# Block-causal attention with a gated convolution unit: q and k loads split in 112 and 16 partitions, and a new hand-written order

## The chip, the cores and the metric

The kernel runs on one core of a Trainium2 chip. The core has five engines that run side by side, each through its own list of instructions in order: TensorE (PE, matmuls; PEld is its weight load), VectorE (DVE), ScalarE (ACT), GpSimd (POOL) and SyncE (SP). Here SP issues nearly all DMAs. The engines wait for each other by semaphores. The metric is the device time of one execution in microseconds, as the median of the runs shown.

## What is computed

Attention over 8 batches, 8 heads, 576 positions and head size 64, where position i sees every position in its own block of 64 and in earlier blocks; then a gated unit on the joined heads (512 columns): a causal convolution of five taps gives a gate, a matrix gives a value, and a second matrix projects gate times value.

```python
scores = scale * np.matmul(q, k.transpose(0, 1, 3, 2))
mask = block_i >= block_j
attn = softmax(np.where(mask, scores, -1e9))
x = np.matmul(attn, v)                      # heads joined: [8, 576, 512]
for t in range(5):
    gate_pre += conv_w[t][None, None, :] * xp[:, t:t + 576, :]
gate = 1.0 / (1.0 + np.exp(-gate_pre))
out = (gate * (x @ w_val)) @ w_out
```

(The softmax is written out in the original; the rest is cut to its core.) Inputs and output are float32; the kernel computes in float16 with float32 sums.

## The kernel before

All work is cut into some 800 steps, and their order is written out by hand as two strings of words, START and PLAN. A loop (`run`, L458) walks through the words and calls one helper for each, so the order of words is the order of instructions on every engine at once: an engine executes those of its own in that order. Nothing is reordered later, and the waits for data and for free buffers follow from the order.

A word is a name, numbers, and behind an @ either the engine (A is ACT, D is DVE, P is POOL) or the PSUM banks. The numbers are a head group Q (0 to 15: batch Q // 2, four heads of it), a batch, or a unit of 512 output rows (8 and 9 are the rests of four batches each).

- `Lq.Q`, `Lk.Q` (L175 to L185) load q or k of a head group, 576 KB on 128 partitions with 4,608 bytes each, into one of three buffers `qks`, so the load for Q needs the casts of Q - 3 done. `Lv.b.c`, `Lvt.b` load v and its tail (256 and 128 KB in pieces of 256 bytes); `Lwv`, `Lwo`, `Lcw` the weights.
- `cq.Q.i` casts k (i = 1) or q (i = 0) to float16; a third number means a part: 0 the first five ninths, 1 the last four. `cv`, `cvt` cast v. `T.Q.i` transposes in blocks of 32 x 32 on DVE.
- `s.Q.t` computes scores (three pieces t per head group), `e.Q.t.a` is exp on ACT, `m` sets the masked corners to zero on POOL; `sl` and `el` do the last rows. `av` multiplies with v on TensorE, `n.Q.a` divides by the sum on DVE.
- x has to be transposed for the second part, in 32 pieces p = 2Q + a, either by `xtr.p` (five TensorE transposes) and `xt.p` (a copy out of PSUM), or by `dx.p`, a DMA that transposes, issued by SP. `tt` copies the ends.
- `cn` (80 small matmuls) is the convolution, `th` its tanh, `val`, `gv` and `o` value, gating and projection, `oc` the copy out of PSUM and `st` the store, issued by SP.
- `w` is a filler matmul on zeros, put where TensorE would wait.

SP walks through loads, `dx` and stores in the order of the words. So a load that stands behind a store is issued only when that store's data is there.

The load of q and k before (L175 to L179):

```python
def load_qk(i, src, Q, m):
    b, g = divmod(Q, 2)
    eng(m, nc.sync).dma_start(
        out=qks[Q % NQS][0:128, i],
        in_=src[b, 4 * g:4 * g + 4].rearrange("h (i n) d -> (h i) (n d)", n=18))
```

Of the kernel before, what the change touches and what calls it, by code (L numbers as in the profile page):

```python
# [19 lines left out]
el.0.1 s.1.0@0123 e.1.1.1 av.0.0@67 cq.2.1@P e.1.0.0 n.0.0 e.1.0.1 s.1.2@0145 m.1.1 cq.2.0@P T.2.1  # L20
av.0.1@67 e.1.2.1 xtr.0@2 e.1.2.0 m.1.0 T.2.0 cq.3.1@P xt.0@A n.0.1 w@3 w@3 w@3 s.2.1@0145 m.1.2
cq.3.0@P av.1.1@23 e.2.1.0 T.3.1 Lq.4 Lwv.0 e.2.1.1 s.2.2@0167 n.1.1 Lv.1.3 e.2.2.1 av.1.0@45 m.2.1
Lv.1.2 T.3.0 e.2.2.0 s.2.0@2367 n.1.0 cv.1.0@P e.2.0.1 xtr.3@0 xtr.1@1 xt.3@D xtr.2@4 e.2.0.0 m.2.2
xt.1@D xt.2@D w@5 sl.1@0167 cq.4.0@P s.3.0@2345 el.1.1 Lvt.1 el.1.0 e.3.0.0 cn.0@0167 Lk.4 tt.0
wv.0@D Lwo.1 wv.2@P T.4.0 e.3.0.1 Lq.5 val.0.0@2 Lwo.0 wv.3@A wv.1@D Lwo.3 m.2.0 m.3.0 Lk.5
val.0.1@3 th.0.0 cv.1.1@P Lwo.2 Lv.3.1 th.0.1 s.3.2@0145 gv.0.0 Lv.2.0 cvt.1@P gv.0.1 e.3.2.1
av.2.0@67 cq.4.1@P e.3.2.0 av.2.1@23 n.2.0 s.3.1@0145 m.3.2 n.2.1 xtr.4@6 e.3.1.0 val.0.3@7 cq.5.0@P
T.4.1 e.3.1.1 xtr.5@2 val.0.2@3 gv.0.3 xt.4@A m.3.1 xt.5@D s.4.1@0145 gv.0.2 av.3.1@67 e.4.1.1 T.5.0
cq.5.1@P Lv.2.1 e.4.1.0 s.4.2@2345 n.3.1 e.4.2.1 av.3.0@01 Lq.6 wo.0@D wo.1@P Lk.7 e.4.2.0 T.5.1
Lvt.2 s.4.0@4567 Lk.6 m.4.1 n.3.0 xtr.7@2 Lv.2.2 m.4.2 e.4.0.1 o.0.3@3 Lv.2.3 e.4.0.0 xt.7@D  # L30
sl.2@0167 oc.0.3@D cv.2.0@P o.0.1@2 el.2.0 el.2.1 xtr.6@3 m.4.0 oc.0.1@A s.5.2@0145 xt.6@D cq.6.0@P
cn.1@2367 e.5.2.1 e.5.2.0 tt.1 T.6.0 val.1.2@4 cq.7.1@P th.1.1 o.0.2@5 th.1.0 m.5.2 Lv.4.0 gv.1.2
cvt.2@P s.5.0@0167 T.7.1 oc.0.2@A cq.6.1@P val.1.0@4 Lv.3.0 e.5.0.0 val.1.1@5 gv.1.0 e.5.0.1 Lq.7
T.6.1 s.5.1@0123 Lk.8 cv.2.1@P val.1.3@4 Lv.3.3 e.5.1.0 gv.1.1 st.0.3 m.5.0 av.4.0@67 Lk.9 e.5.1.1
gv.1.3 Lv.4.3 s.6.1@0145 n.4.0 m.5.1 cv.3.0@P av.5.0@23 e.6.1.0 xtr.8@6 e.6.1.1 n.5.0 o.1.3@7
cq.7.0@P xt.8@A s.6.2@0145 oc.1.3@D st.0.1 xtr.10@2 m.6.1 e.6.2.0 T.7.0 Lvt.3 o.1.2@3 cq.8.1@P Lvt.4
xt.10@A s.6.0@0167 oc.1.2@D e.6.2.1 o.1.1@2 T.8.1 e.6.0.0 m.6.2 av.5.1@45 oc.1.1@D Lv.5.1 e.6.0.1
av.4.1@01 n.5.1 cq.9.1@P s.7.2@2367 n.4.1 Lq.8 o.1.0@4 e.7.2.0 m.6.0 st.0.2 Lv.4.2 xtr.9@5 e.7.2.1
oc.1.0@D s.7.1@0123 cvt.3@P Lv.3.2 xt.9@D xtr.11@4 cvt.4@P e.7.1.1 o.0.0@5 xt.11@D m.7.2 tt.2
e.7.1.0 sl.3@2367 oc.0.0@D el.3.1 T.9.1 s.7.0@0145 m.7.1 el.3.0 cn.2@2367 e.7.0.0 Lq.9 cq.8.0@P  # L40
Lv.4.1 e.7.0.1 val.2.0@0 Lk.10 T.8.0 th.2.0 Lv.5.0 m.7.0 cv.4.1@P val.2.2@1 th.2.1 gv.2.0 s.8.1@2345
cv.3.1@P val.2.3@0 gv.2.2 e.8.1.1 Lq.11 av.7.0@67 st.1.3 e.8.1.0 gv.2.3 cq.9.0@P st.1.2 s.8.2@0145
Lq.10 n.7.0 Lv.5.3 av.6.1@23 e.8.2.1 cv.4.0@P T.9.0 av.6.0@67 e.8.2.0 m.8.1 Lk.11 n.6.1 cq.10.1@P
dx.14 sl.4@0145 n.6.0 el.4.0 el.4.1 m.8.2 s.9.2@0123 val.2.1@4 T.10.1 e.9.2.0 dx.12 av.7.1@67
cq.11.0@P e.9.2.1 gv.2.1 s.8.0@0145 n.7.1 cv.5.0@P o.2.0@2 e.8.0.1 T.11.0 m.9.2 o.2.2@3 e.8.0.0
dx.15 cq.10.0@P oc.2.0@D s.9.1@4567 Lk.13 oc.2.2@A xtr.13@0 e.9.1.1 o.2.1@1 xt.13@D m.8.0 T.10.0
e.9.1.0 s.9.0@2367 Lv.6.2 oc.2.1@D e.9.0.0 cq.11.1@P av.8.1@45 e.9.0.1 Lv.5.2 s.10.0@0123 n.8.1
m.9.1 e.10.0.0 av.8.0@67 m.9.0 T.11.1 e.10.0.1 s.10.1@0145 tt.3 n.8.0 e.10.1.1 av.9.1@23 m.10.0
# [1 line left out]
st.2.2 cv.5.1@P val.3.0@1 Lk.12 th.3.0 gv.3.3 Lvt.5 cn.8@2367 Lv.7.1 gv.3.0 st.0.0 val.3.1@0 Lq.14  # L50
th.8.1 th.8.0 s.11.1@4567 gv.3.1 val.8.1@1 e.11.1.1 Lv.7.0 val.3.2@0 gv.8.1 e.11.1.0 cq.12.0@P
s.11.0@2367 gv.3.2 o.2.3@1 e.11.0.1 m.11.1 T.12.0 o.3.2@0 e.11.0.0 cq.12.1@P Lk.14 oc.2.3@D
sl.5@4567 oc.3.2@A dx.19 av.9.0@23 el.5.1 st.2.3 el.5.0 cvt.5@P T.12.1 s.10.2@0167 Lq.13 m.11.0
o.3.3@4 e.10.2.0 n.9.0 o.3.1@5 e.10.2.1 Lvt.7 T.13.1 s.11.2@0123 dx.18 oc.3.1@A cq.14.0@P val.8.2@6
oc.3.3@D e.11.2.1 val.8.0@5 gv.8.2 val.8.3@4 m.10.2 e.11.2.0 gv.8.0 s.12.1@2367 T.14.0 Lv.6.3
e.12.1.0 av.10.1@01 m.11.2 gv.8.3 cq.14.1@P e.12.1.1 av.11.1@45 n.10.1 s.12.0@2367 m.12.1 T.14.1
o.8.0@0 e.12.0.0 dx.16 n.11.1 o.8.1@1 e.12.0.1 cq.13.0@P dx.21 oc.8.0@D s.14.0@2345 oc.8.1@A Lv.6.0
av.11.0@67 e.14.0.1 m.12.0 T.13.0 o.3.0@0 e.14.0.0 st.8.1 n.11.0 cv.6.1@P Lv.7.3 av.10.0@45 oc.3.0@A
m.14.0 sl.6@2367 tt.4 n.10.0 dx.22 cv.7.0@P el.6.1 el.6.0 s.14.2@0167 dx.23 cn.4@2345 cvt.7@P
e.14.2.0 dx.20 e.14.2.1 val.4.1@0 Lv.7.2 th.4.0 m.14.2 val.4.3@1 th.4.1 gv.4.1 s.13.1@2367 Lv.6.1  # L60
# [7 lines left out]
el.7.1 s.15.1@0145 dx.26 n.13.1 o.5.1@6 e.15.1.1 dx.27 o.5.0@7 e.15.1.0 oc.5.1@D s.15.0@2345 st.5.1
oc.5.0@D m.15.1 av.14.1@01 e.15.0.0 st.5.0 av.14.0@67 e.15.0.1 n.14.1 tt.6 val.6.3@2 n.14.0 m.15.0
dx.29 av.15.1@01 dx.28 av.15.0@45 n.15.1 val.6.1@3 n.15.0 dx.31 cn.6@0167 dx.30 val.6.0@4 th.6.1  # L70
val.6.2@5 th.6.0 gv.6.3 o.5.2@6 gv.6.2 tt.7 gv.6.0 val.7.1@2 oc.5.2@A gv.6.1 val.9.0@7 st.5.2
val.9.3@3 cn.9@0145 o.6.3@6 th.9.1 th.9.0 gv.9.3 o.6.0@4 oc.6.3@A gv.9.0 val.9.2@3 st.6.3 oc.6.0@A
val.9.1@5 gv.9.2 val.7.2@4 st.6.0 gv.9.1 cn.7@0167 o.6.2@3 th.7.1 val.7.3@5 th.7.0 oc.6.2@D gv.7.2
# [432 lines left out]
```

## Time and profile before

| what | value |
|---|---|
| time, median of three runs | 186.37 us (185.02 to 187.07) |
| the profiled execution | 184.9 us, of which the span is 183.1 us |
| instructions in the span | 6,862, of them 2,938 matmuls and as many weight loads |
| granted TensorE clock, mean | 0.987 |
| moved by DMA | 43.41 MB, 237 GB/s on average |
| loads of q and k | 32 of 576 KB, in the median 6.8 (q) and 7.3 us (k) from issue to landing |
| stores | 35 of 256 KB, in the median 4.5 us |
| DMA transposes of x | 19, in the median 4.2 us |

The span is the time between the first and the last instruction of the profile. Of the page's rows, those with 40 digits show the span in equal slices, each digit the busy share in tenths. The chain of waits follows the work that ended last backwards, at each step to what released it. "Issue" is time in which an engine waited for nothing that the profile shows. A row of the timeline has start, duration, engine, line, operation, and in brackets the idle time just before with what ended it.

### The profile page before, as it was taken

How to read it: one execution, taken by the hardware profiler on the slowest of the kernel's cores; microseconds unless marked ns; L12 is line 12 of the kernel's file. 1: busy time of each engine (PE TensorE's matmuls, PEld its weight loads, DVE VectorE, ACT ScalarE, POOL GpSimd, SP SyncE). 2: the span in 40 equal slices, each digit the busy share in tenths (PEclk: the TensorE clock that was granted, in tenths of full speed). 3: DMA queues.
4: the chain of work that ended last, by engine and by line, in shares of the span. 5: the costliest groups of instructions: out<-in, count | busy, mean ns of one | idle time of the engine just before them, and what ended most of it. 6: DMA issues, size and time to landing. Idle time of an engine off the chain costs nothing.

```text
span 183.1 us, 6862 instructions
## 1 busy us (share of the span) xinstructions
PE 159.1 (87%) x2938; PEld 91.8 (50%) x2938; DVE 114.8 (63%) x182; ACT 130.6 (71%) x160; POOL 87.4 (48%) x150
## 2 busy tenths in 40 slices
PE   7885877696969999798989977899998996999991
PEld 2533665274533765376366444664533754745540
DVE  6850785579638796689885439973454874455510
ACT  3498869779669887987897867689889564054461
POOL 7387565965494656687926155743417301000000
PEclk9999699999999999999999999999999999999998
DMA  6999999999999999999996999999997296552255
GB/s 204 368 191 386 341 295 223 294 238 192 314 207 236 346 236 236 297 341 369 171 241 228 306 312 237 299 153 188 275 325 245 91 143 168 107 94 107 75 210 191
DMA packets 61368, 43.41 MB, mean 237 GB/s; under 512 B 51477, under 2 KB 51733, under 8 KB 61338
## 3 DMA queue, kind: packets, MB, share of 16 engines
q1 hardware_dynamic: 61184, 42.84, 91.6%
q8 instruction: 23, 0.38, 0.9%
q10 hardware_dynamic: 154, 0.14, 0.2%
q14 instruction: 7, 0.06, 0.2%
HBM read 30.42 MB, written 9.44 MB: 218 GB/s over the span
## 4 chain that ended last, share of the span: by engine, by line
PE 41%; ACT 18%; DMA 11%; POOL 8%; issue 8%; DVE 6%; SPq 5%; POOLq 0%; DVEq 0%; ACTq 0%
PE PS L115 40%; ACT pt L264 15%; POOL qk L172 5%; DMA xt<-x 4%; DMA vst<-in_v_dram 4%; DMA qks<-in_q_dram 3%; DVE qkT L236 2%; DVE gv L381 2%; SPq L413 2%; ACT th L363 2%; SPq L193 1%; DVE x L314 1%; SPq L177 1%; POOL pt L281 1%; POOL w_val L227 1%
## 5 line engine op out<-in xcount | busy, mean ns | idle before, releaser
L264 ACT ACTIVATE pt<-PS 128x1024 f16<-128x1024 f32 x96 | 93.1, 1025 | 24.4 <-PE PS L115 14.7
L172 POOL CAST qk<-qks 128x1152 f16<-128x1152 f32 x30 | 45.2, 1511 | 18.2 <-DMA qks<-in_q_dram 6.1
L236 DVE STREAM_TRANSPOSE qkT<-qk 128x576 f32<-128x576 f32 (+2 forms) x34 | 39.1, 1159 | 12.9 <-POOL qk L172 12.8
L115 PE MATMUL PS<-qkT 32*128 32x64 f16 (+4 forms) x768 | 34.3, 278 | 7.6 <-ACT pt L264 4.0
L115 PE MATMUL PS<-v,pt 128*128 128x65 f16 x896 | 34.6, 196 | 6.9 <-ACT pt L264 2.2
L115 PEld LDWEIGHTS <-pt 128*128 128x128 f16 x960 | 32.9, 99 | 14.9 <-issue 7.7
L381 DVE SCALAR_TENSOR_TENSOR gv<-th,PS 128x512 f16<-128x512 f32 (+1 forms) x40 | 26.6, 693 | 18.1 <-ACT th L363 13.9
L115 PE MATMUL PS<-w_out,gv 128*128 128x512 f16 x144 | 34.8, 380 | 0.1
L115 PE MATMUL PS<-xt,w_val 128*128 128x512 f16 x128 | 31.7, 380 | 2.0 <-DMA xt<-x 1.3
L115 PEld LDWEIGHTS <-qkT 32*128 32x128 f16 x768 | 15.6, 93 | 26.2 <-issue 19.4
L363 ACT ACTIVATE th<-PS 128x1024 f32<-128x1024 f32 (+1 forms) x20 | 17.7, 940 | 14.8 <-PE PS L115 13.8
L314 DVE TENSOR_TENSOR x<-PS,rc 128x640 f16<-128x640 f32 x32 | 26.4, 825 | 1.2
L115 PEld LDWEIGHTS <-w_val 128*128 128x128 f16 x160 | 14.1, 97 | 15.7 <-issue 3.5
L115 PEld LDWEIGHTS <-gv 128*128 128x128 f16 x144 | 12.9, 98 | 15.6 <-issue 2.8
L281 POOL MEMSET pt<- 64x128 f32 x32 | 6.3, 200 | 27.7 <-ACT pt L264 24.6
L172 POOL CAST v<-vst 128x1024 f16<-128x1024 f32 x16 | 16.6, 1047 | 2.2 <-DMA vst<-in_v_dram 1.7
L313 DVE RECIPROCAL rc<-PS 128x10 f32<-128x10 f32 x32 | 6.5, 205 | 16.6 <-PE PS L115 14.7
L172 DVE COPY osb<-PS 128x512 f32<-128x512 f32 x17 | 11.5, 683 | 7.0 <-PE PS L115 4.4
L172 ACT COPY osb<-PS 128x512 f32<-128x512 f32 x18 | 10.6, 587 | 4.0 <-PE PS L115 4.0
L115 PE MATMUL PS<-xt,DG 32*32 32x512 f16 x640 | 11.5, 377 | 1.4 <-issue 1.4
L115 PE MATMUL PS<-v16t,pt 128*128 128x65 f16 x64 | 12.5, 195 | 0.1
L115 PEld LDWEIGHTS <-DG 32*32 32x32 f16 x800 | 9.0, 88 | 6.0 <-issue 4.6
...
## 6 DMA issues: line engine op xcount, KB each, us to landing
...
xt<-x SPq DMA_TRANSPOSE x19, 4.2
```

Of the source, the lines that this page charges most:

```text
L115: nc.tensor.matmul(out=out, lhsT=lhsT, rhs=rhs, start=start, stop=stop, skip_group_check=True)
L172: (e.copy if e is nc.scalar else e.tensor_copy)(out=o, in_=i)
L177: eng(m, nc.sync).dma_start(out=qks[Q % NQS][0:128, i], in_=src[b, 4 * g:4 * g + 4].rearrange("h (i n) d -> (h i) (n d)", n=18))
L193: eng(m, nc.sync).dma_start(out=vtst[b % 2][0:64, 0:8, 0:64], in_=v[b, 0:8, 512:576].rearrange("h s d -> s h d"))
L236: nc.vector.transpose(out=qkT[Q % NQT][0:128, i].bitcast(fp32)[:, :, 0:288] .rearrange("p a (i n) -> p n a i", n=9)[:, n], in_=qk16[Q % NQ ...
L264: nc.scalar.activation(out=pts[Q % NPT][0:128, 2 * a:2 * a + 2, 512 * t:512 * t + 512], in_=PS[0:128, k0:k0 + 2], func=AF.Exp, bias=0.0, s ...
L281: nc.gpsimd.memset(p[64:128, 0:4, 256 * t:256 * t + 32], 0.0)
L313: nc.vector.reciprocal(out=rc[0:128], in_=O[:, :, :, 64:65])
L314: nc.vector.tensor_tensor(out=x16[p % NX16][0:128].rearrange("p i h d -> p h i d"), in0=O[:, :, :, 0:64], in1=rc[0:128].to_broadcast([128, ...
L363: nc.scalar.activation(out=ths[UO.index(n) % NTH][0:128, 2 * r:2 * r + 2, 0:w], in_=PS[0:128, k0:k0 + 2, 0:w], func=AF.Tanh, bias=0.0, sca ...
L381: nc.vector.scalar_tensor_tensor(out=o, in0=t, scalar=1.0, in1=u, op0=ALU.add, op1=ALU.mult)
L413: eng(m, nc.sync).dma_start(out=rows, in_=lay(osb[slot[n, t]]))
```

## The change

Each load of q and k is issued as two DMAs, of partitions 0 to 111 and 112 to 127. START and PLAN are replaced by a new order. Counted over both orders:

| steps | before | after |
|---|---|---|
| DMAs issued for q and k | 32 | 64 |
| `dx` (DMA transposes of x) | 19 | 15 |
| `xtr` with `xt` (TensorE transposes of x) | 13 | 17 |
| `w` (filler matmuls) | 33 | 39 |

The pieces of x that change their way are 14, 15, 17, 18 and 22 (to TensorE) and 10 (to DMA). One part cast of the first k goes from DVE to POOL; some copies out of PSUM and casts of weights go to another engine. All else is the same steps in another order. Head group 3 now comes before 2 in loads and casts, for instance, and stores stand elsewhere among the loads.

```diff
 START = """
-Lk.0 Lq.0
+Lq.0 Lk.0
 """
 
 PLAN = """
-Lcw z.0 Lk.1 Lq.1 Lv.0.1 z.2 Lvt.0 z.1 Lv.0.0 cq.0.1.0@A cq.0.1.1@D w@7 w@7 w@7 w@7 w@7 w@7 w@7 w@7
-w@7 cw@0 T.0.1.1 T.0.1.0 cq.0.0.0@A cq.0.0.1@D cT T.0.0.1 T.0.0.0 cq.1.1@P DG w@4 w@4 w@4 w@4 w@4
-w@4 w@4 w@4 s.0.1@0123 e.0.1.0 Lv.0.2 cq.1.0@P T.1.1 e.0.1.1 w@6 w@6 w@6 w@6 s.0.0@0145 Lv.0.3
...
-dx.17 e.10.1.0 st.2.0 cq.13.1@P cn.3@4567 n.9.1 st.1.1 st.1.0 st.2.1 m.10.1 val.3.3@0 Lq.12 th.3.1
...
-val.4.2@0 e.13.1.1 gv.4.3 val.4.0@1 e.13.1.0 gv.4.2 st.3.2 st.3.1 s.14.1@4567 gv.4.0 tt.5 st.8.0
-m.13.1 Lq.15 cn.5@0123 e.14.1.1 st.3.3 cv.7.1@P Lk.15 e.14.1.0 st.3.0 o.4.3@6 Lvt.6 cv.6.0@P th.5.0
...
+Lvt.0 Lcw z.0 z.2 Lq.1 z.1 Lk.1 w@7 w@7 w@7 w@7 w@7 w@7 w@7 w@7 w@7 cw@0 Lv.0.0 cvt.0@P Lv.0.1
+cq.0.0.0@A cq.0.0.1@D cT T.0.0.1 DG cq.0.1.0@A cq.0.1.1@P T.0.1.1 cq.1.0@P T.0.1.0 Lq.3 T.0.0.0 Lk.3
+T.1.0 cq.1.1@P w@4 w@4 w@4 w@4 w@4 w@4 w@4 w@4 w@4 w@4 w@4 w@4 w@4 w@4 w@4 w@4 w@4 s.0.0@0123 Lv.0.3
+e.0.0.0 Lv.0.2 T.1.1 e.0.0.1 w@6 w@6 w@6 w@6 s.0.1@0145 cv.0.0@P e.0.1.1 m.0.0 e.0.1.0 w@6 w@6 w@6
...
+th.2.0 val.2.0@2 Lv.7.1 xt.15@D m.8.1 Lv.6.0 th.2.1 val.2.2@3 gv.2.1 cv.5.1@P gv.2.0 sl.4@0167
+val.2.3@4 gv.2.2 el.4.0 tt.3 el.4.1 T.11.1 s.10.2@0123 val.3.2@5 cq.11.0@P e.10.2.0 gv.2.3 st.0.1
+st.0.2 e.10.2.1 cn.3@0167 Lq.12 T.11.0 cq.12.1@P Lq.14 val.3.1@4 th.3.0 m.10.2 Lv.6.1 Lv.6.3 o.2.3@2
...
+dx.19 T.13.0 el.5.0 cvt.6@P el.5.1 s.12.2@2367 m.12.0 oc.3.2@A st.8.0 o.3.0@1 e.12.2.0 Lvt.7
+av.10.1@45 oc.3.0@D e.12.2.1 s.11.1@0123 n.10.1 st.3.2 m.12.2 av.10.0@67 Lk.15 e.11.1.1 cq.13.1@P
+Lq.15 e.11.1.0 s.11.2@2345 st.3.0 n.10.0 e.11.2.1 o.8.1@0 m.11.1 dx.21 T.13.1 dx.20 e.11.2.0
...
 """
...
     def load_qk(i, src, Q, m):
         b, g = divmod(Q, 2)
-        eng(m, nc.sync).dma_start(
-            out=qks[Q % NQS][0:128, i],
-            in_=src[b, 4 * g:4 * g + 4].rearrange("h (i n) d -> (h i) (n d)", n=18))
+        rows = src[b, 4 * g:4 * g + 4].rearrange("h (i n) d -> (h i) (n d)", n=18)
+        for p in (slice(0, 112), slice(112, 128)):
+            eng(m, nc.sync).dma_start(out=qks[Q % NQS][p, i], in_=rows[p])
```

More of the change, by code (lines that the diff above doesn't have):

```diff
@@ L20 @@
[L20 to L48, printed above, removed]
-dx.17 e.10.1.0 st.2.0 cq.13.1@P cn.3@4567 n.9.1 st.1.1 st.1.0 st.2.1 m.10.1 val.3.3@0 Lq.12 th.3.1
@@ L50 @@
[L50 to L60, printed above, removed]
-val.4.2@0 e.13.1.1 gv.4.3 val.4.0@1 e.13.1.0 gv.4.2 st.3.2 st.3.1 s.14.1@4567 gv.4.0 tt.5 st.8.0
@@ L68 @@
[L68 to L73, printed above, removed]
@@ new lines @@
+n.1.0 e.2.2.1 s.2.0@0123 Lv.1.0 m.3.1 e.2.0.0 m.2.2 sl.1@4567 cvt.1@P el.1.0 xtr.2@0 el.1.1 xtr.3@1
+e.2.0.1 xt.2@D s.3.2@4567 xt.3@D cq.4.1@P e.3.2.1 cn.0@0123 Lwo.3 Lk.6 e.3.2.0 tt.0 T.4.1 val.0.0@6
+Lwo.1 cq.4.0@P th.0.1 Lv.2.2 val.0.3@7 Lv.2.3 th.0.0 cv.1.1@P T.4.0 s.3.0@2345 val.0.2@0 cv.1.0@P
+e.3.0.1 gv.0.0 val.0.1@1 gv.0.3 e.3.0.0 m.2.0 m.3.2 gv.0.2 s.2.1@4567 Lwo.0 gv.0.1 m.3.0 cq.6.1@P
+av.3.0@23 Lwo.2 e.2.1.1 Lq.6 e.2.1.0 n.3.0 s.4.2@0167 Lv.3.0 Lv.2.1 e.4.2.0 av.3.1@45 m.2.1 T.6.1
+e.4.2.1 xtr.6@0 cv.2.1@P n.3.1 av.2.0@23 xt.6@A m.4.2 xtr.7@1 n.2.0 s.4.0@4567 wo.1@A wo.0@P Lq.5
@@ new lines @@
+xt.7@D xtr.4@0 e.4.0.1 av.2.1@23 Lk.5 xt.4@D cq.6.0@P e.4.0.0 o.0.0@0 Lk.7 n.2.1 m.4.0 s.4.1@4567
+Lv.3.3 oc.0.0@A T.6.0 Lvt.2 xtr.5@1 e.4.1.0 Lv.3.1 o.0.3@0 cv.2.0@P xt.5@D e.4.1.1 s.6.2@2345 tt.1
+oc.0.3@D o.0.2@1 cq.5.0@P e.6.2.0 o.0.1@0 e.6.2.1 oc.0.2@D m.4.1 cq.5.1@P T.5.0 s.6.1@2367 oc.0.1@A
+e.6.1.1 Lq.9 cn.1@0145 m.6.2 T.5.1 cq.7.1@P e.6.1.0 Lq.7 val.1.0@6 Lq.8 th.1.0 m.6.1 cvt.2@P
+val.1.3@7 Lv.3.2 th.1.1 gv.1.0 Lv.4.0 sl.2@0123 cv.3.0@P val.1.1@6 gv.1.3 el.2.1 el.2.0 T.7.1
+s.5.1@0123 cq.9.0@P val.1.2@7 e.5.1.1 gv.1.1 av.4.0@45 e.5.1.0 gv.1.2 cq.7.0@P s.6.0@2367 Lv.4.3
@@ new lines @@
+n.4.0 av.4.1@01 e.6.0.1 m.5.1 cq.8.0@P T.7.0 st.0.0 e.6.0.0 Lq.10 s.5.0@4567 n.4.1 Lvt.3 cv.3.1@P
+e.5.0.0 xtr.8@2 Lk.8 o.1.2@3 xt.8@D e.5.0.1 m.6.0 Lv.5.1 s.5.2@0145 oc.1.2@D Lv.5.0 o.1.3@2 m.5.0
+e.5.2.0 T.8.0 xtr.9@3 e.5.2.1 s.7.1@0167 oc.1.3@D xt.9@D e.7.1.1 m.5.2 sl.3@2345 cq.10.0@P T.9.0
+el.3.0 el.3.1 s.7.0@2367 st.1.2 e.7.1.0 av.5.1@45 cvt.3@P st.0.3 Lk.10 e.7.0.0 m.7.1 cq.8.1@P
+av.5.0@01 n.5.1 Lv.4.1 e.7.0.1 Lv.4.2 o.1.1@2 n.5.0 m.7.0 s.7.2@4567 oc.1.1@A T.8.1 xtr.11@3 e.7.2.0
+av.6.0@01 xt.11@D e.7.2.1 T.10.0 s.8.0@2345 dx.10 e.8.0.1 av.6.1@67 m.7.2 n.6.0 Lk.9 cq.10.1@P
@@ new lines @@
+th.3.1 gv.3.1 val.8.3@3 gv.3.2 s.9.2@0167 oc.2.3@A val.3.3@4 e.9.2.1 o.2.2@2 gv.3.3 e.9.2.0
+cq.12.0@P cn.8@4567 Lvt.4 oc.2.2@D st.1.1 m.9.2 Lk.14 val.8.1@2 cq.14.0@P th.8.1 o.2.1@0 th.8.0
+st.1.3 gv.8.3 Lv.7.2 s.9.0@4567 gv.8.1 oc.2.1@A Lv.7.0 val.3.0@1 e.9.0.0 val.8.2@0 cvt.4@P e.9.0.1
+gv.3.0 s.9.1@2345 gv.8.2 val.8.0@1 e.9.1.0 m.9.0 T.12.0 av.8.1@67 Lq.13 e.9.1.1 gv.8.0 cq.14.1@P
+o.2.0@0 st.1.0 n.8.1 Lv.6.2 s.10.0@2345 oc.2.0@A Lvt.6 m.9.1 o.3.1@1 T.12.1 e.10.0.0 Lvt.5 xtr.17@0
+e.10.0.1 oc.3.1@D s.10.1@2367 xt.17@D e.10.1.1 av.9.0@45 m.10.0 st.2.1 e.10.1.0 cq.13.0@P st.2.2
@@ new lines @@
+sl.6@2367 o.3.3@4 m.11.0 el.6.0 el.6.1 cn.4@2367 oc.3.3@A cq.15.1@P st.3.3 av.11.1@45 cq.15.0@P
+th.4.0 th.4.1 n.11.1 av.11.0@23 gv.4.2 s.13.2@4567 dx.23 cv.7.1@P gv.4.0 val.4.1@1 e.13.2.1 cv.7.0@P
+n.11.0 val.4.3@0 e.13.2.0 cvt.7@P gv.4.1 xtr.22@2 gv.4.3 s.12.1@4567 m.13.2 xt.22@A tt.5 cn.5@0123
+e.12.1.1 T.15.0 e.12.1.0 T.15.1 o.4.1@6 th.5.0 m.12.1 o.4.2@7 oc.4.1@D th.5.1 s.13.1@0145 st.4.1
+oc.4.2@D val.5.0@6 e.13.1.0 st.4.2 o.4.3@7 e.13.1.1 gv.5.0 sl.7@0123 oc.4.3@D val.5.1@6 m.13.1
+el.7.1 el.7.0 st.4.3 s.14.0@0123 gv.5.1 val.5.2@7 e.14.0.0 av.12.1@45 e.14.0.1 gv.5.2 s.13.0@0167
```

32 lines of the change are left out of this document (22 added, 10 removed).

## The prediction

> **What bounds the kernel now.** I read the page first, then busy time by stretch, the chain of waits, and TensorE's timeline where the chain stands still.
>
> ```profile
> PE 159.1 (87%) x2938; PEld 91.8 (50%) x2938; DVE 114.8 (63%) x182; ACT 130.6 (71%) x160; POOL 87.4 (48%) x150
> ...
> PE   7885877696969999798989977899998996999991
> ...
> DMA  6999999999999999999996999999997296552255
> ...
> q8 instruction: 23, 0.38, 0.9%
> ```
>
> TensorE is the busiest engine, but two things hide in its 87%: it is under 90% in most of the first third, and the DMA engines are full until about 140 us. So the early and middle stages are a race between loads and compute, and only the last third is TensorE alone. Queue q8 brings TensorE's own instructions: 5,876 matmuls and weight loads in 23 packets, some 256 each.
>
> ```profile
> 10.00:20.00 10.00, 7.32 (x118) 3.88 (x118) 3.56 (x5) 8.97 (x11) 6.54 (x11) 0.90 1.17 312
> 40.00:50.00 10.00, 8.15 (x143) 4.92 (x142) 8.64 (x13) 7.92 (x11) 4.67 (x9) 1.00 1.12 241
> 110.00:120.00 10.00, 8.48 (x129) 5.18 (x130) 9.85 (x16) 7.17 (x9) 5.87 (x10) 1.00 1.38 261
> ```
>
> (Columns: stretch, length, busy PE, PEld, DVE, ACT, POOL, granted clock, DMA share, GB/s.) Summed over all such rows TensorE idles 19.0 us between 10 and 180: 9.7 before 60, 2.7 in 100 to 120, 0.9 in 140 to 150, 1.7 in 150 to 160, 0.8 at the very end. That is what a better order could win at most, besides some 4 us of filler matmuls after the first scores.
>
> ```profile
> 44.31 0.34 PE L115 MATMUL PS<-v,pt 128*128 128x65 f16 x6 [0.30 <-ACT pt L264]
> 46.20 0.41 PE L115 MATMUL PS<-v,pt 128*128 128x65 f16 x8 [1.55 <-issue]
> ...
> 50.84 0.96 PE L115 MATMUL PS<-xt,DG 32*32 32x512 f16 x46
> 53.21 0.82 PE L115 MATMUL PS<-xt,DG 32*32 32x512 f16 x34 [1.41 <-issue]
> ```
>
> Two stops in the middle of one group of like matmuls, waiting for "issue", 256 instructions apart. The trace's packets of q8 that run from 43.41 and 50.36 for 1.31 and 1.43 us end just as the stops begin, and TensorE goes on 1.4 to 1.5 us later. It had run out of instructions: the packets were asked for when the block before began (37.8 and 46.2) and started 5.6 and 4.2 us later, behind data. Both stops are on the chain.
>
> ```profile
> 96.64 2.24 SPq L413
> 98.88 0.04 issue
> 98.93 0.43 SPq L413
> 99.36 0.04 issue
> 99.40 5.13 DMA qks<-in_q_dram
> 104.53 0.05 issue
> 104.59 1.48 POOL qk L172
> ```
>
> Here the load of q 12 stands on SP behind stores, is issued at 99.40, and its cast on POOL waits for the landing.
>
> **The change part by part**, against the profiled run: 184.9 us, of which 183.1 are the span; the median of three runs is 1.5 higher, 186.4.
>
> *Later start, +2.0.* Before, the first scores start at 8.28 and the first exp at 8.94. Now s.0.0 needs cq.0.1.1, which went from DVE (0.45 us) to POOL, behind cvt.0 and so behind the landing of Lvt.0. Loads land about 1.5 us apart at first (k 0 at 4.98, q 0 at about 6.4, by the casts that waited). So the tail of v lands at about 7.3; cvt.0 takes 0.62, four ninths of a POOL cast of 1.51 take 0.67, and three half transposes (0.64, 0.73, 0.73) follow: scores at about 10.7, +2.5. The 17 filler matmuls now right in front (8 before, 5.75 to 7.65), at 1.90/8 us, end at 9.8, +1.5. I take the middle, as ACT is 90% busy from 10 to 20 and carries a late start along.
>
> *Instruction stops, -3.0.* Counting the plan's matmuls in blocks of 256 instructions and adding the sizes of the transfers in each, blocks 2 to 16 hold 0 to 3.6 MB before (0.0, 1.7, 3.3, 0.3, 2.4, 3.0, 0.8, ...) and 1.5 to 2.6 MB after. No block piles up loads; but SP runs ahead of the plan's places as far as buffers allow, so this spreads only partly. Both stops gone are -2.96, and two stretched groups (0.88 us at 37.4 and 0.75 at 81.6, against 0.6) add some 0.4 that I don't count. The other bound is two further stops of this length, +3.
>
> *Late q and k, -3.3.* Lq.12 stood behind dx.17, st.2.0, st.1.1, st.1.0 and st.2.1; now behind st.0.1 and st.0.2, whose data was ready five blocks earlier. Lq.15 and Lk.15 (issued at 130.5 and 132.8, cast on the chain at 137.4 and 140.2) stood behind st.3.2, st.3.1 and st.8.0; now they are two blocks earlier, behind st.3.2 alone. I count 2.4 of the 2.7 us of idle TensorE in 100 to 120 and the 0.9 in 140 to 150. Against it: the median place of a load is 183 TensorE instructions ahead of its cast instead of 239. If that decides, the other q and k come later instead: POOL's waits for them are 12.0 us now, and a quarter more, all of it on the path, would be +3.
>
> *Four transposes of x from DMA to TensorE, +1.4.* dx 14, 15, 17, 18 and 22 become xtr and xt, xtr.10 becomes dx.10. A group of five transposes takes 0.28 to 0.44 us on TensorE; four of 0.35 make 1.4, counted whole since TensorE is about 90% busy there. Five evacuations more on DVE (0.451 each) lie under its 37% of idle time, and ACT loses one of 0.64. SP loses four issues of 1.23.
>
> *The split, +0.6.* 32 more issues on SP, each 0.40 to 0.46 us when nothing is in the way: 13.8, less 4.9 for the transposes. SP issues for 139.8 us of the span, mostly held up by its queue; its share of the chain is 5% (9.2 us), so 6.6% of its time shows: 0.6. What is queued behind each extra issue are the next loads, and their casts on POOL. The issue records also show eight completion semaphores used in turn, an issue waiting for the landing eight transfers back; two per load mean fewer bytes in flight, so later loads but a shorter queue ahead of q8. The bounds are nothing at all and all 8.9; below nothing if the shorter queue outweighs it, by at most the 0.6 us of the stretched groups and the 2.96 already counted. The extra landing that each cast waits for follows the first by one issue, 0.43, covered where loads land early.
>
> [...]
>
> *Other moves* (engines of output evacuations, weights to ACT and POOL): the same work on engines that are 48% to 71% busy; nothing. The filler matmuls lie in waits; those before the first scores are in the start.
>
> Sum: +2.0 - 3.0 - 3.3 + 1.4 + 0.6 = -2.3, so 182.6 for a run like the profiled one, 184.1 for the median.
>
> [...]
>
> **Rivals.**
>
> *It balances: 186.4.* TensorE has the same work behind the last norm in both plans (now from 158 to 179 us, 228 matmuls in 15.6 us of it at the end of the chain), and from 60 to 180 it is 92% busy. If the late start is +2.5 and only 2.4 of each of the two gains comes, what is left is 2.5 + 1.4 + 0.9 - 4.8 = 0. For it: ACT, too, has the same work up to the last norm. Against it: idle time before 60 that is no start.
>
> *The stops only move: 188.9.* Blocks 3 to 5 still last 6 us by their rows, and a packet took up to 5.6 + 1.3 + 1.5 = 8.4 us from request to use. If the DMA engines stay full, it stops elsewhere: +2.5 + 1.4 + 0.6, -2.0 for q and k, 0 for stops, is +2.5. It decides if q8 packets still start over 4 us late with blocks under 7 us. Against: q and k take two of eight places in flight.
>
> *The split drags the loads: 190.7.* Slower is the sign here. The DMA engines are full until 140 us; if a piece of 16 partitions costs them or SP 0.43 us that nothing covers, 32 make 13.8; a third on the path, 4.6, with the start 2.0, transposes 1.4, q and k -0.7 and stops -3.0, is +4.3. It decides where SP, not a buffer, releases the loads; 5% of the chain says that is rare, 183 instructions instead of 239 that it is less rare now.
>
> **How the numbers follow.** Measured times of this kernel spread by 1.1%, so 1% either way is no change. Forecast 0.42; balance 0.20; moved stops 0.21; dragging split 0.17. So faster 0.42, same 0.20, slower 0.38, and the time is the likeliest case's, 184.1. Its own range is 180.5 (start at 1.5, no price for the split, the stretched groups, all 3.6 of late q and k, and 1.8 us of the idle time before 60: 0.5 + 0.6 + 0.4 + 0.3 + 1.8 less) to 184.5. The range runs to 190.5, the edge of the last rival; 2 in 10 lie outside, mostly above.
>
> **What would show it.** First exp at 10.3 to 11.5 us. No TensorE "issue" stop over 1 us in mid-group. POOL's waits for q and k well below 12 us, no load in 100 to 120 landing on the chain. SP issues 161 transfers; its share of the chain stays near 5%. I am wrong if DMA stays full past 145 us, if TensorE idles over 10 us before 60, or if q and k casts wait longer than now.

## The result, and the profile after

| | before | after |
|---|---|---|
| time, median of 4 runs each | 185.69 us | 210.56 us (209.56 to 211.24) |
| the profiled execution, and its span | 184.9, 183.1 us | 211.24, 209.5 us |
| TensorE busy, and not busy, in the span | 159.1, 24.0 us | 176.5, 33.0 us |
| granted TensorE clock, mean | 0.987 | 0.915 |
| moved by DMA | 43.41 MB, 237 GB/s | 42.77 MB, 204 GB/s |
| first exp starts, last division by the sum | 8.94, 158.2 us | 12.82, 184.3 us |

The ratio is 1.133, with a 95% interval of 1.123 to 1.142: the change makes the kernel 13% slower. (Some executions of a kernel take over 1.5% more than its fastest; ratios and intervals leave those out, medians keep them, so a ratio can differ a little from the quotient of two medians.) The forecast was 184.1 us, and the range ended at 190.5. The page of the changed kernel, with the rows that were shown of before:

```profile
PE 176.5 (84%) x2964; PEld 100.8 (48%) x2964; DVE 115.4 (55%) x184; ACT 131.9 (63%) x160; POOL 88.7 (42%) x152
...
PE   7994858969589886796986599879899999999992
...
PEclk9999797996958997599999579996999999999998
DMA  6999999999999999999999999999990427591255
...
q8 instruction: 23, 0.38, 0.9%
...
DMA 36%; PE 28%; SPq 14%; ACT 11%; issue 5%; POOL 3%; DVE 1%; ACTq 0%; POOLq 0%; DVEq 0%
```

Three things are to be read here. The DMA row is full until about 157 us; before it was full until about 140, and slightly fewer bytes are moved now. So the same loads keep the DMA engines busy longer. DMA and SP's queue (SPq) make up half of the chain, where they were 16% before. And PEclk, the granted clock in tenths of full speed, has 5s, 6s and 7s up to some 147 us. The waits of the engines of the changed kernel (engine, line and tile, what it waited for, us in total, times, longest):

```profile
DVE qkT L236 <- POOL qk L172: 28.2, 17, 3.8
...
POOL qk L172 <- DMA qks<-in_q_dram: 22.1, 15, 3.8
...
POOL qk L172 <- DMA qks<-in_k_dram: 16.6, 12, 2.3
```

And the steps of its chain of waits, up to 80 us, that are landings of q or k (start, duration, what):

```profile
2.11 6.11 DMA qks<-in_k_dram
...
15.63 10.76 DMA qks<-in_q_dram
...
34.66 7.25 DMA qks<-in_q_dram
...
70.41 8.15 DMA qks<-in_q_dram
```

POOL now waits 38.7 us for q and k; before it was 12.0. DVE, which transposes what POOL has cast, waits 28.2 (12.8 before). Four landings of q or k stand on the chain before 80 us, the longest of 10.76 us.

That explains idle engines, but TensorE is also *busy* for 17.4 us more with nearly the same matmuls (2,964, 26 more). Where that comes from is seen around one stop, first in the timeline of TensorE:

```profile
110.58 1.03 PE L115 MATMUL PS<-w_out,gv 128*128 128x512 f16 x4
...
113.19 1.02 PE L115 MATMUL PS<-xt,w_val 128*128 128x512 f16 x4 [0.60 <-DVE gv L381]
117.53 1.86 PE L115 MATMUL PS<-w_out,gv 128*128 128x512 f16 x4 [3.32 <-ACT osb L172]
```

The instruction that TensorE waited for, in the timeline of ACT:

```profile
116.89 0.58 ACT L172 COPY osb<-PS 128x512 f32<-128x512 f32 x1 [5.14 <-DMA out_dram<-osb]
```

And busy time by stretch (length, busy PE, PEld, DVE, ACT, POOL, granted clock, DMA share, GB/s):

```profile
108.00:112.00 4.00, 4.00 (x99) 2.04 (x100) 0.60 (x1) 2.58 (x3) 1.86 (x3) 1.00 1.10 242
112.00:116.00 4.00, 1.61 (x21) 0.78 (x21) 2.41 (x4) 0.00 (x0) 1.80 (x3) 0.97 1.09 256
116.00:120.00 4.00, 2.47 (x58) 0.99 (x57) 0.57 (x1) 2.43 (x3) 0.65 (x1) 0.50 1.07 278
120.00:124.00 4.00, 4.00 (x67) 1.80 (x51) 1.42 (x3) 2.00 (x4) 2.68 (x4) 0.68 1.01 199
```

TensorE stops for 3.32 us because ACT has waited 5.14 us for a store, which must free the buffer that ACT copies into. From 116 to 120 the granted clock is 0.50, and four projection matmuls that took 1.03 us at 110.58 take 1.86. In the clock's records 0.50 begins at 115.75 us, while TensorE stands, and lasts for 6.83 us. There are seven such stretches before 150 us, of 3.41 or 6.83 us each; before the change there is one, and with the new order but whole loads one too. In the 3.41 us before 115.75 TensorE was busy for 1.27, and for 0.9 to 2.0 us in the 3.41 us before each of the other six. So a late transfer was paid for twice here: as a stop of 3.32 us, and as slow matmuls after it, 1.86 us in place of 1.03.

### The profile page after: what moved, and what is told of

It is laid out like the page before. It is cut to its first block, busy times and chain, and to the rows that moved or that the text cites. A ratio compares the mean times of both kernels' runs of the same rounds, so it can differ in the third digit from the quotient of the medians.

```text
span 209.5 us, 6951 instructions
## 1 busy us (share of the span) xinstructions
PE 176.5 (84%) x2964; PEld 100.8 (48%) x2964; DVE 115.4 (55%) x184; ACT 131.9 (63%) x160; POOL 88.7 (42%) x152
## 2 busy tenths in 40 slices
DMA packets 59193, 42.77 MB, mean 204 GB/s; under 512 B 49301, under 2 KB 49557, under 8 KB 59162
## 4 chain that ended last, share of the span: by engine, by line
DMA 36%; PE 28%; SPq 14%; ACT 11%; issue 5%; POOL 3%; DVE 1%; ACTq 0%; POOLq 0%; DVEq 0%
PE PS L115 28%; DMA qks<-in_q_dram 12%; DMA xt<-x 9%; ACT pt L264 8%; SPq L179 6%; DMA out_dram<-osb 6%; SPq L188 4%; DMA vst<-in_v_dram 3%; DMA th<-in_moe_w_out_dram 3%; DMA qks<-in_k_dram 3%; SPq L413 2%; SPq L202 2%; ACT th L363 1%; POOL qk L172 1%; POOL v L172 1%
## 5 line engine op out<-in xcount | busy, mean ns | idle before, releaser
L172 POOL CAST qk<-qks 128x1152 f16<-128x1152 f32 (+1 forms) x31 | 45.1, 1456 | 38.9 <-DMA qks<-in_q_dram 22.1
L236 DVE STREAM_TRANSPOSE qkT<-qk 128x576 f32<-128x576 f32 (+2 forms) x34 | 38.6, 1154 | 29.1 <-POOL qk L172 28.2
L115 PE MATMUL PS<-qkT 32*128 32x64 f16 (+4 forms) x768 | 37.5, 298 | 13.4 <-ACT pt L264 5.7
L115 PE MATMUL PS<-w_out,gv 128*128 128x512 f16 x144 | 39.6, 412 | 6.3 <-ACT osb L172 3.3
L115 PEld LDWEIGHTS <-pt 128*128 128x128 f16 x960 | 34.9, 102 | 8.2 <-issue 5.2
L115 PE MATMUL PS<-v,pt 128*128 128x65 f16 x896 | 36.2, 200 | 2.2 <-ACT pt L264 0.8
L381 DVE SCALAR_TENSOR_TENSOR gv<-th,PS 128x512 f16<-128x512 f32 (+1 forms) x40 | 25.8, 694 | 15.1 <-ACT th L363 9.9
L115 PEld LDWEIGHTS <-qkT 32*128 32x128 f16 x768 | 17.0, 98 | 34.9 <-issue 28.3
L115 PEld LDWEIGHTS <-gv 128*128 128x128 f16 x144 | 13.9, 104 | 22.8 <-issue 11.6
L172 ACT COPY osb<-PS 128x512 f32<-128x512 f32 x18 | 10.5, 586 | 15.5 <-DMA out_dram<-osb 8.4
L115 PE MATMUL PS<-wz 128*128 128x512 f16 x39 | 13.7, 515 | 1.2 <-DVE tiny L466 1.2
L115 PE MATMUL PS<-v16t,pt 128*128 128x65 f16 x64 | 12.8, 200 | 0.0
L115 PEld LDWEIGHTS <-DG 32*32 32x32 f16 x800 | 9.6, 88 | 5.2 <-issue 3.5
```

What stands on the lines that cost most here:

```text
L115: nc.tensor.matmul(out=out, lhsT=lhsT, rhs=rhs, start=start, stop=stop, skip_group_check=True)
L172: (e.copy if e is nc.scalar else e.tensor_copy)(out=o, in_=i)
L236: nc.vector.transpose(out=qkT[Q % NQT][0:128, i].bitcast(fp32)[:, :, 0:288] .rearrange("p a (i n) -> p n a i", n=9)[:, n], in_=qk16[Q % NQ ...
L381: nc.vector.scalar_tensor_tensor(out=o, in0=t, scalar=1.0, in1=u, op0=ALU.add, op1=ALU.mult)
```

## The experiments

Theory and rivals were these. *Split*: the two pieces of a load cost the DMA engines far more than one whole, and the rest of the chain is late because of it. *Count*: it is the number of DMAs that costs, whatever their shape. *Order*: the new order itself makes the loads late. Ratios are to runs of the kernel before on the same chip, with 95% intervals.

### Which half of the change costs

The split alone, in the old order (START and PLAN of before):

```diff
-            out=qks[Q % NQS][0:128, i],
-            in_=src[b, 4 * g:4 * g + 4].rearrange("h (i n) d -> (h i) (n d)", n=18))
+        for p in (slice(0, 112), slice(112, 128)):
+            eng(m, nc.sync).dma_start(out=qks[Q % NQS][p, i], in_=rows[p])
```

> The order of before, with each load of q and k issued as 112 and 16 partitions and nothing else changed. Theory A (the split makes the transfers themselves slow: the 4,608-byte packets, in the median 179 ns before, are 275 ns in the changed kernel): most of the 25 us are here, 202 to 214 us, and the median packet is above 240 ns. Theory B (two DMAs per load cost it, by SP's issues and places in flight, whatever their shape): also 202 to 214, but the packets stay near 180 ns. Theory C (the new order costs it): 184 to 190.

The order alone: START and PLAN of after, and `load_qk` of before, so the same diff backwards.

> The order of after, with each load of q and k as one DMA of 128 partitions. Theory A and B: the loss is gone; by the prediction's sum without the 0.6 for the split, 2.9 us below before, 182 to 185. Theory C: above 200.

The new order with two DMAs per load that are no split of partitions: both reach all 128, with half of the bytes of each.

```diff
-        for p in (slice(0, 112), slice(112, 128)):
-            eng(m, nc.sync).dma_start(out=qks[Q % NQS][p, i], in_=rows[p])
+        for c in (slice(0, 576), slice(576, 1152)):
+            eng(m, nc.sync).dma_start(out=qks[Q % NQS][0:128, i, c], in_=rows[:, c])
```

> The order of after, each load of q and k as two DMAs, but of all 128 partitions and half of the bytes of each (2,304). The same number of DMAs, issues and semaphores as after. Theory A (the shape over the partitions): within 3 us of the order-only run. Theory B (the number of DMAs): 205 or more.

And the loads by themselves: attention and the gated unit are left out, and the kernel only loads pieces of q, in stages of six loads each, with a copy on DVE as a barrier between the stages.

> Attention and the gated unit are left out; the kernel only loads the first six groups of q, again and again, in nine stages with a barrier between: whole; 112 and 16 partitions; 112 alone; 16 alone (112 to 127); whole in two halves of the bytes; 64 and 64; 96 and 32; 16 partitions eight apart; whole again. Theory A: whole and halves move at 380 GB/s or more, some 9 us a stage of 3.5 MB; 112 and 16 needs 13 us or more. If neighbouring partitions share a way into SBUF, 16 alone is slow for its bytes and the 16 that lie eight apart take about half as long in the packets; 64 and 64 is then as slow as 112 and 16 or slower. Theory B: 112 and 16, halves, 64 and 64 and 96 and 32 all cost about the same, and their packets run at the pace of whole ones. [...]

| kernel | median us | ratio | packets of q and k, median |
|---|---|---|---|
| split only | 206.97 | 1.122 [1.094, 1.151] | 265 ns |
| order only | 188.32 | 1.027 [1.012, 1.041] | 180 ns |
| order, halves by bytes | 192.49 | 1.049 [1.035, 1.062] | 93 ns (2,304 bytes each) |
| after | 210.56 | 1.133 [1.123, 1.142] | 274.5 ns |

A packet is the record of one descriptor of 4,608 bytes, one partition's share of a load; in the trace of before its median is 179 ns. The split alone costs 12%, the order alone some 2% (it was expected at 182 to 185 us, faster than before). The count of DMAs is the smaller part: as many of them in another shape cost 2 points over the order alone (4.2 us, where at most 3 were expected), in place of 10.6. Most of the time goes with the duration of a packet. The sum of the durations of all data packets is 161 us for each of the 16 DMA engines with the order alone, 168 with the halves, and 193 with the split (packets can overlap: the DMA share above goes up to 1.10). Of the 32 us between the first and the last, 18 are the packets of q and k; 10 are those of 256 bytes (v and the transposes of x), which are loaded as before and get slower beside them (18 ns in the median before the change, 22 after it).

The loads by themselves, each stage's rate from its first packet to its last:

| stage | median packet | GB/s |
|---|---|---|
| whole, 128 partitions | 178 ns | 338 |
| 112 and 16 | 291 ns | 242 |
| 112 alone, 16 alone | 248, 271 ns | 271, 129 |
| halves by bytes | 93 ns | 328 |
| 64 and 64 | 332 ns | 227 |
| 96 and 32 | 299 ns | 239 |
| 16 partitions, eight apart | 274 ns | 109 |
| whole, again | | 326 |

Busy time by stretch of that kernel, for the stages whole, 112 and 16, halves, 64 and 64 (the third last column is TensorE's clock, then DMA share and GB/s; the edges of a stage are in it, so the rates differ a little from the table):

```profile
2.00:12.00 10.00, 0.00 (x0) 0.00 (x0) 1.00 0.90 352
14.00:29.50 15.50, 0.00 (x0) 0.00 (x0) 1.00 0.89 228
...
50.00:61.00 11.00, 0.00 (x0) 0.00 (x0) 1.00 0.91 321
62.50:79.50 17.00, 0.00 (x0) 0.00 (x0) 1.00 0.90 208
```

The DMA share is 0.89 to 0.91 in all four: the engines are equally occupied and move 352 or 208 GB/s. So this is neither SP's issue rate nor a queue that runs empty. A split at 64, into two equal pieces, is no better than one at 112, so it is not the small size of the 16 either. 64 and 64 takes 1.5 times as long as whole (15.6 against 10.5 us). Two things came out otherwise than expected: whole moves 338 GB/s and not 380, and the packets to 16 neighbours are no longer than those to 16 that lie eight apart (271 and 274 ns). But the two stages of 16 move 0.44 MB each, in 3.4 and 4.1 us; the next kernel will show that this is too short.

For the kernel this can be turned into an estimate: six split loads take 14.60 us from the first packet to the last, six whole ones 10.46. That is 0.69 us of all 16 engines per load, or 22 us for 32 loads, if nothing else is in the way.

### Why a packet gets longer

What the slow pieces share is that their partitions are neighbours, fewer than 128 of them. Each stage here is one shape again (attention and gated unit left out): `buf[lo:hi:step]` with the same number of partitions, once as neighbours and once spread over all 128.

> Attention and the gated unit are left out; only loads of q, in seven stages with a barrier between: 32 neighbouring partitions; 32 that lie four apart; 64 neighbours; 64 that lie two apart; all 128; 16 neighbours; 16 that lie eight apart. All stages but the last two move 3.5 MB. Theory P (neighbouring partitions share a way into SBUF, so that the engines of one DMA get into each other's way): neighbours move at about 200 GB/s, the spread ones of the same number at 280 or more, whole at 330; packets of neighbours 300 ns or more in the median, of spread ones below 240. Theory Q (any DMA of fewer than 128 partitions is slow, or the reading side is): neighbours and spread ones of the same number are equal within 10%. [...]

| stage | median packet | GB/s |
|---|---|---|
| 32 neighbours | 361 ns | 205 |
| 32, four apart | 178 ns | 225 |
| 64 neighbours | 355 ns | 206 |
| 64, two apart | 178 ns | 310 |
| whole | 178 ns | 341 |
| 16 neighbours | 675 ns | 115 |
| 16, eight apart | 268 ns | 117 |

The 64 neighbours and the 64 two apart, as one sees them in the timeline of DVE in that kernel: the barrier's copies, with the wait for the last landing of the stage in brackets. The first of the two is of the third row, the second of the fourth; 3.54 MB are moved in each.

```profile
58.15 0.27 DVE L46 COPY buf<-zero 128x24 f32<-128x24 f32 x2 [19.57 <-DMA buf<-in_q_dram]
71.60 0.27 DVE L46 COPY buf<-zero 128x24 f32<-128x24 f32 x2 [13.18 <-DMA buf<-in_q_dram]
```

The same bytes to the same number of partitions take 19.57 or 13.18 us, and a packet takes twice as long to 64 neighbours as to 64 that are two apart, or to 32 neighbours as to 32 that are four apart; to 16 neighbours it takes 3.8 times as long as to all 128. The packets to 16 neighbours get there only with time: the first 96 take 254 and 333 ns (medians of 48), the rest 675, and the stage of 16 in the kernel above ended after 96. (With 32 partitions four apart and 16 eight apart SP's issues, 0.59 us each without a pause, hold the engines up, at DMA shares of some 0.7 and 0.4; there the packets tell, not the rates. Why packets to 16 eight apart take 268 ns and not 178 is open.)

Why neighbours get longer packets is not shown. That they share a way into SBUF was the author's theory P, and the difference between neighbours and spread partitions is what it expected. But spread partitions also read spread rows of q, since the index stands on both sides of the load, so the reading side was not separated from the writing side. 32 and 64 neighbours run alike (361 and 355 ns), though their rows span different lengths, and the 112 partitions of the larger piece alone ran at 248 ns and 271 GB/s. What is shown is that the shape over the partitions makes the packets long: 178 ns to 64 partitions two apart, 355 to 64 neighbours.

The same in the whole kernel: the new order with two DMAs per load, of the 64 even and the 64 odd partitions.

```diff
-        for p in (slice(0, 112), slice(112, 128)):
+        for p in (slice(0, 128, 2), slice(1, 128, 2)):
```

> The changed kernel with each load of q and k cut into the 64 even and the 64 odd partitions instead of 112 and 16. The same number of DMAs, issues and semaphores. In the loads alone 64 partitions that lie two apart ran at 310 GB/s with packets of 178 ns, neighbours at 206 with 355 ns. If the shape over the partitions is the 8% that the split by 112 and 16 costs above the split by bytes: within 2% of that kernel (192.5 us, 4.85% above before), so 189 to 197, median packet below 200 ns. If any cut across the partitions costs it: 205 or more.

Measured: 197.25 us, just above what was expected, 1.071 [1.062, 1.079], with packets of 178 ns again and a sum of 165 us per engine, near the 161 of the order alone. The same 64 DMAs of the same bytes cost 7% in this shape and 13% as 112 and 16: 6 points go with the shape. It is 2 points above the halves by bytes. One difference stands in the traces: an issue of 64 spread partitions takes SP 0.59 us in the median, one of half the bytes 0.43, which is some 10 us more for 64 issues, and SP's queue is 23% of the chain against 8%. That this makes the 2 points was not tested.

### What the order costs

The order alone gave 1.027 [1.012, 1.041]. It was run once more for a second interval:

> The order-only kernel once more, on the same chip as the two with its repairs, so that they are compared side by side. 2% to 3.5% above before, as in the first run of it.

188.64 us, 1.014 [1.006, 1.023], a little less than expected. So the order costs 1.4 to 2.7%. Its page (first run), with TensorE's clock and the DMA row:

```profile
PE 161.8 (87%) x2964; PEld 94.4 (51%) x2964; DVE 115.8 (62%) x184; ACT 130.7 (70%) x160; POOL 88.8 (48%) x152
...
PEclk9999699999999999999999999999999999999999
DMA  6999999897999999999999999999413276941265
```

And its chain of waits around 100 us:

```profile
92.75 4.47 DMA out_dram<-osb
...
97.30 0.59 ACT osb L172
...
97.94 0.87 PE PS L115 x4
...
101.14 6.04 DMA out_dram<-osb
```

TensorE is not busy for 185.9 - 161.8 = 24.1 us, as before the change (24.0); in the second run it is 25.7. It is busy for 2.7 us more, with 20 transposes of x and 6 filler matmuls more. So the order moved the idle time rather than shortened it: two waits for stores (4.47 and 6.04 us) now stand on the chain around 100 us. Six kernels tried to win the 2% back by moving words of the order.

*The start nearly as before*: cq.0.1.1 on DVE again, Lvt.0 behind Lk.1, cvt.0 behind the casts of group 1, eight fillers in place of 17.

```diff
-Lvt.0 Lcw z.0 z.2 Lq.1 z.1 Lk.1 ... Lv.0.0 cvt.0@P Lv.0.1 ... cq.0.1.0@A cq.0.1.1@P
+Lcw z.0 z.2 Lq.1 z.1 Lk.1 Lvt.0 ... Lv.0.0 Lv.0.1 ... cq.0.1.0@A cq.0.1.1@D ... cvt.0@P
```

> The order-only kernel (2.65% above before; first exp at 11.9 us instead of 8.9, last norm 2.5 us later) with its start put back: the tail of v is loaded behind k 1, cvt.0 stands behind the casts of group 1, cq.0.1.1 is on DVE again, DG stands behind the first transposes, 8 filler matmuls instead of 17. Theory D (the late start is carried to the end): first exp at 9.5 or earlier and 2 to 3 us less, at most 1.3% above before. Theory E (loads of v and stores that come late in the middle set the time): first exp as early, but within 1 us of the order-only kernel, 2% or more above before.

190.6 us, 1.023 [1.014, 1.031]. The first exp starts at 9.38 in place of 11.88 us, and nothing of it shows at the end: the ratio lies between the two of the order alone.

*Four stores earlier*, so that ACT's and DVE's output buffers come free:

```diff
-cvt.3@P st.0.3 Lk.10 ... gv.2.3 st.0.1 st.0.2 ... oc.2.2@D st.1.1 ... th.8.0 st.1.3
+cvt.3@P st.0.3 st.0.2 st.0.1 Lk.10 ... gv.2.3 st.1.1 st.1.3 ... oc.2.2@D ... th.8.0
```

> The order-only kernel with four stores moved forward: st.0.2 and st.0.1 right behind st.0.3, st.1.1 and st.1.3 to where those two stood. In the order-only kernel ACT's copies oc.2.3 and its successors wait 5.9 us for buffers that these stores still hold, on the chain at 92 to 97 and 101 to 107 us. Theory F (the late stores are what the new order gives back): ACT's waits for stores fall below 1 us and the time by 2 to 4 us, to within 1% of before. Theory G (loads of v and the late start still set the time): the waits go, the time stays within 1 us of the order-only kernel.

189.58 us, 1.025 [1.017, 1.033]: ACT's wait for stores (5.9 us) is gone, and the time is no shorter.

*Both together*:

> Both repairs in the order-only kernel: the start as in the kernel with the repaired start, and the four stores moved forward. Theory D and F together: 4 to 6 us less than the order-only kernel, 1% to 2% below before. If each gain is eaten by the next load that comes late: within 1% of the order-only kernel.

187.6 us, 1.016 [1.008, 1.024], no different from the order alone.

*Five pieces of x back on DMA* (the prediction had counted four more on TensorE, one having gone the other way, as 1.4 us of cost):

```diff
-xtr.14@7 ... xt.14@D
+dx.14
```

and so for 15, 17, 18 and 22.

> The new order with loads of 128 partitions, and the pieces 14, 15, 17, 18 and 22 of x transposed by DMA again, as before the change (piece 10 stays a DMA transpose too). Theory G, the order costs what TensorE and the evacuations do more: TensorE's busy time falls by about 1.8 us (five groups of 0.35), and the ratio to before falls from 1.0144 to 1.0265 to about 1.005 to 1.015. Theory H, the order costs by its many late landings: five more transfers on SP among loads and stores; the ratio stays at 1.014 to 1.03, and more waits for DMA appear on the chain.

The *loads of q and k that stood far behind* the cast that frees their buffer, moved half as far behind it (by the words that change place there are 16):

> The new order with loads of 128 partitions, and 17 loads of q and k that stood over 60 steps behind the last cast of their buffer's occupant put half as far behind it. Theory H, the order costs by late landings of q and k: POOL's waits for them fall from 13 to 16 us to below 8, and the ratio from 1.0144 to 1.0265 to 1.01 or less. Rival, as in the run that moved four loads of the old order forward: stores, v and instruction packets come later instead, waits for v and for stores grow by some us, and the ratio is 1.02 or more.

And *start, stores and x together*:

> The new order with loads of 128 partitions, the old start, the four stores early, and the five pieces of x back on DMA. If the cost of the order is a sum of these three places, the ratio is 1.00 to 1.008. If it lies in the order as a whole (which head group is computed when), it stays at 1.015 to 1.025, though first exp comes at about 9.8 us and ACT waits under 1 us for stores.

The medians are 195.61, 198.11 and 193.07 us, beside 186.02 for the kernel before in 11 runs. Those runs spread from 181.35 to 192.31 us, so no interval is given; the quotients of the medians are 1.05, 1.06 and 1.04. All three are slower than the order alone. For the x pieces and for the three together that is more than either theory expected; for the loads it is what the rival expected. With x on DMA TensorE waits for a DMA transpose, in the timeline:

```profile
90.31 0.96 PE L115 MATMUL PS<-xt,w_val 128*128 128x512 f16 x3 [0.65 <-DMA xt<-x]
95.70 0.58 PE L115 MATMUL PS<-xt,w_val 128*128 128x512 f16 x1 [4.42 <-DMA xt<-x]
```

4.42 us in the middle of a group, and the granted clock from 70 to 100 us is 0.89. With the earlier loads POOL's waits for q and k are as short as expected (1.2 us), but TensorE stops for 6.00 us at 49.2: it needs the output weights, which landed late because SP stood for 5.62 us before it could issue one of their loads.

### The old order, with single terms of the prediction

*Loads of q and k first.* The third term said that Lq.12 and Lq.15 come too late behind stores. Here, in the kernel before:

```diff
-dx.17 e.10.1.0 st.2.0 ... val.3.3@0 Lq.12 ... Lk.12 ... st.3.2 st.3.1 ... Lq.15 ... Lk.15
+Lq.12 Lk.12 dx.17 e.10.1.0 st.2.0 ... val.3.3@0 ... Lq.15 Lk.15 st.3.2 st.3.1 ...
```

> The order of before, with only Lq.12 and Lk.12 moved in front of dx.17 and the stores behind it, and Lq.15 and Lk.15 in front of st.3.2 and st.3.1. It tests the prediction's third term alone. If that term was right: 2 to 3 us less than before (ratio 0.984 to 0.99). If other work was the limit there: within 0.7 us (0.996 to 1.004).

190.0 us, 1.028 [1.020, 1.036]: slower, which neither theory expected. In the timeline of TensorE:

```profile
101.26 0.44 PE L115 MATMUL PS<-xtt,DG 32*32 32x256 f16 x31
104.37 0.72 PE L115 MATMUL PS<-xtt,DG 32*32 32x256 f16 x49 [2.67 <-issue]
```

A group of 80 like matmuls is cut in two by 2.67 us of "issue". The packet with its next instructions started at 102.18 us, 4.4 us after the block before it began, with some 240 packets of q and k served in between. Later, at 138.6, TensorE stops for 4.16 us: DVE waits for a store, which now stands behind the other two loads.

*Instruction blocks moved.* 17 filler matmuls of the kernel before are cut in four, at the same width in sum. So all later borders of the blocks of 256 instructions fall 102 instructions earlier in the work.

```diff
-        mm(f32(m[0]), wz[0:128, 0:128], wz[0:128])
+        n = 4 if m[0] in (4, 7) else 1
+        for c in range(0, 512, 512 // n):
+            mm(f32(m[0])[:, c:c + 512 // n], wz[0:128, 0:128], wz[0:128, c:c + 512 // n])
```

> The order of before; the 17 filler matmuls ahead of the first scores are each cut into four of 128 columns, so that 102 more instructions stand there and every border of a 256-instruction block moves by that much; nothing else. It tests the prediction's second term. If the two stops for instructions (1.55 and 1.41 us) hang on where the borders fall and are carried to the end: both gone and 2 to 3 us less, or moved and no change. If what follows them has slack: both gone and within 1 us of before.

> The old order with the borders of the instruction blocks moved, repeated beside the two other kernels. It was 1.0048 [0.9995, 1.0101]; the same again, within 1 per cent of before, says that the two instruction stops are worth at most 1 us.

183.73 us, 1.005 [1.000, 1.010], and 182.66 us, 0.997 [0.987, 1.007]. Both stops in mid-group are gone, and the time is the same within 1%. In the first profile another stop of 1.58 us stands in mid-group at 95.2; in the second none is over 0.52 us.

*The five pieces of x on TensorE in the old order*, alone and with the moved blocks, as the search for a version better than both:

```diff
-dx.14 sl.4@0145 n.6.0 el.4.0 el.4.1
+xtr.14@2 sl.4@0145 n.6.0 el.4.0 xt.14@D el.4.1
```

and so for 15, 17, 18 and 22.

> The old order and whole loads, with the pieces 14, 15, 17, 18 and 22 of x transposed by TensorE in place of a DMA (six to one steps of the order later copied out of PSUM by DVE). In the new order the reverse cost some 7 us. Theory K, that edit is a gain wherever SP has loads, stores and transposes in one queue: the load of q 12, which stood behind the DMA transpose of piece 17, is issued earlier, and the ratio to before is 0.98 to 0.995. Rival, the gain is one of the new order alone (there pieces 14 and 15 are used a few steps after): TensorE's 1.75 us more work shows, ratio 1.00 to 1.01.

> As the run beside it, with the borders of the instruction blocks moved by 102 instructions (17 filler matmuls cut in four). If both edits gain and add up, the ratio is 0.97 to 0.99; if only the borders matter, as alone (0.9995 to 1.0101); if the transposes cost, 1.00 to 1.015.

189.37 us, 1.038 [1.029, 1.046], and 187.99 us, 1.032 [1.026, 1.039]: 3 to 4% slower, more than any of the expectations. In the chain of the first stand three stops for instructions:

```profile
46.13 2.10 issue
...
83.51 1.44 issue
...
105.29 1.71 issue
```

The first is that of before, in the same group of matmuls, with 2.10 in place of 1.55 us; the other two are new. They are no explanation by themselves, since the second kernel has none of over 1 us and costs as much. No version tried is faster than the kernel before by more than the noise.

## Why the prediction was wrong

*The split, +0.6: this step failed.* The order alone ends its span at 185.9 us and the order with the split at 209.5, so the term is 23.6 us by these two spans, and some 20 to 22 by the ratios (1.133 against 1.014 to 1.027); it was bounded by 0 and 8.9. The bounds came from SP: so many issues of 0.43 us, and the share of them on the chain. That the pieces would cost the DMA engines nothing was taken for granted. The runs give them a price: 4,096 packets take 274.5 in place of 180 ns, and with the same order the DMA row stays full until about 157 in place of 130 us. The estimate from the loads alone, 22 us, is near the whole term, but not all of the term is packets: with as many DMAs and packets at full speed 2 to 6 of the 11 to 12 points remain (halves, even and odd), and 6 to 8 points, some 11 to 16 us, go with the long packets. Of the 23.6 us, 8.9 are more idle time of TensorE (33.0 against 24.1) and 14.7 are more busy time for the same 2,964 matmuls (176.5 against 161.8), as the granted clock is 0.915 in place of 0.990; in the old order, in one trace, the split brings 13.4 of idle and 9.0 of busy time. The clock was in none of the terms. The rival in which the split drags the loads had the sign and the place; its price, a third of 13.8, was a fifth of what was measured.

*Later start, +2.0: right in place, undersized, and not carried.* Scores were put at +1.5 to +2.5 us. The first exp is 2.94 us later with the order alone and 3.88 with both (the forecast band ended at 11.5, it came at 12.82). But putting the old start back gained nothing that shows at the end, so counting it whole was wrong: later waits absorb it.

*Instruction stops, -3.0: they went, their worth did not follow.* No stop of TensorE for instructions is left, as forecast, with the order alone too. The old order without its two stops is as fast as with them (1.005, with one other stop in its profile, and 0.997). So the term is within 1% of nothing, about 1.8 us either way, though both stops stood on the chain.

*Late q and k, -3.3: wrong sign for the simple remedy.* With the order alone POOL waits 13.1 us for q and k (12.0 before), and 38.7 with the split. Loads moved forward in the old order, and others in the new, made the kernel slower, as stores, weights and instructions were late in their place.

*Four transposes, +1.4: the work is there, the price is not.* TensorE is busy for 2.7 us more with the order alone, fillers included. But five such moves in the old order cost 3 to 4% (1.038 and 1.032), and their reverse in the new one costs some 7 us (195.61 beside 188.3 to 188.6, on different chips), so 1.4 is right for neither.

*Signs named beforehand.* DMA stays full past 145 us, TensorE idles for 12 us between 10 and 60 (over 10 was named) and POOL waits longer for q and k: all that was to show the forecast wrong is there. SPq is 14% of the chain, not 5%. Two slips in the working change nothing: the stretched groups add 0.4 us, and a bound takes 0.6; the rival that balances takes 0.9 us that has no source (with the split's 0.6 it comes to -0.3).

What stays open is what the 1.4 to 2.7% of the order is made of. It is not its start, its stores, its x pieces or its loads singly: undoing or moving each gave nothing or lost more.
